# An mLSTM layer and its gated MLP on one core: score banks 2 and 3 for 2 and 5, an early table load, opening decays in three pieces, another order

## The chip, the cores and the metric

The program runs on one core of a Trainium2 chip. A core has five engines that run side by side and meet at semaphores: TensorE (PE in the profile; its weight loads are PEld), VectorE (DVE), ScalarE (ACT), GpSimd (POOL) and SyncE (SP), which here issues nearly all DMAs. The metric is the device time of one execution in microseconds (us), less is better. TensorE's clock has two levels, 1.2 and 2.4 GHz; the profile shows as "PEclk" which share of full speed was granted.

## The reference

```python
# mLSTM, for 4 batches x 8 heads, 768 tokens, head size 40
m_new = max(f[t] + m, i[t])
f_stab, i_stab = exp(f[t] + m - m_new), exp(i[t] - m_new)
C = f_stab * C + i_stab * outer(v[t], k[t])
n = f_stab * n + i_stab * k[t]
y[t] = sigmoid(o[t]) * (C @ q[t]) / max(abs(n @ q[t]), 1)
# then an MLP over all 3072 tokens: x is y with its 8 heads side by side (320 wide)
h = x @ w_in            # 320 -> 2048
out = (h * sigmoid(h)) @ w_out   # 2048 -> 320
```

## The kernel before

The sequence is cut into 6 chunks of 128 tokens, so there are 24 **units** (chunk c of batch b is unit n = 4c + b). A unit computes the mLSTM of its chunk in matrix form: scores of queries and keys, multiplied ("weighed") by a table of decays, times values, plus queries times the state that the chunk before left. The result is normalised, gated, and transposed into x. The MLP runs in eleven groups: an **opening** for units 0 to 3 (its pieces are called mA, mB and mJ, with tanh, glu and second product beside them), and ten **steps** of two units each, cut into 8 slices. First products are made of bits high and low (xh, xl, wh, wl) in fp32r. The weights come as 64-bit numbers and are put together on ACT and DVE (L329 to L386) before they are of use.

**The order is a table.** Nothing is scheduled at run time: the string ORDER holds some 1,600 words, and perform() calls one function for each, so that every engine gets its instructions in the order of the words. Each engine then runs its own list strictly in order, and an instruction that waits holds up all behind it. The words that matter here, with their lines before:

- z: spins, matmuls of 512 columns whose result nobody reads (L927).
- s, sb: the opening decays of units 0 to 3 in PSUM (spread L526, spans L543 and L553), e: their exponential (L564).
- S: scores (L657), w: weigh, DVE's product of the two score banks with the decay table D (L676), v and P: weighted values and their products with the keys (L594, L621), c: the state carried on (L637 to L643), V and Q: values and queries (L686, L705), g: gate (L722 to L736), x, h, y: transposes and the split into xh and xl (L742, L752, L756).
- m, a, b, f, F, n: a slice's first product (L769), tanh on ACT (L877), glu on DVE (L881), high part on ACT (L888), low part on DVE (L892), second product (L907). In the opening a, b, n are L815, L820, L831.
- qk, kvo, lq, d: the DMAs of a unit's queries and keys (raw, L470), of its keys, values and gate (kvo, L479), of its decays for queries (lq, L502) and of its decay table (D, L490). gs, gu, gm, gt, gf: gates (scan, sub, sum, top, flip), go: their store to DRAM (LFd, L276), from which lq and D are read back. t: tanh of the output gate on ACT (L610), O: a step's output copied from PSUM on ACT (L918), D: the output's DMA (L788).

PSUM has 8 banks of 512 columns. Before, second products gather in banks 0 and 1, first products alternate between banks 3 and 4, a unit's two halves of scores stand in **banks 2 and 5**, its transposes in 2, and banks 6 and 7 hold values, queries and products. The score banks are read by weigh as one operand, made by this function:

```python
def banks(a, b):
    return PS[:, a : b + 1 : b - a, :]     # for (2, 5): PS[:, 2:6:3, :]
```

Of the kernel before, what the change touches and what calls it, by code (L numbers as in the profile page):

```python
# [14 lines left out]
AF = mybir.ActivationFunctionType  # L15
# [40 lines left out]
kvo4 Mi5 Ri3 kvo5 Mo2 mB0 Zi2 k5.1 Ji2 aB0 Ti2 qk4 bB0 Ri2 mJ6 mJ4 lq6 So2 aJ6 Mo3 bJ6 So3 Si5 k5.0 aJ4 k6.0 mB2 aB2 nB0
bJ4 k6.1 e4.1 Zo3 Zo2 bB2 Jo2 mJ7 e4.0 Mc4 Sc4 aJ7 mB1 Li6 Lo5 Lo4 qk5 Zc4 Jo3 kvo6 gs2 aB1 e6.0 Mi4 nB2 l4 nJ4 nJ6 Jc4
bJ7 bB1 Zi5 Si4 Lo6 Lo7 Ji5 Zi4 mB3 Ji4 aB3 Ti5 e5.1 nJ7 Li7 mJ5 gu2 v4 Tc4 S4.0 e5.0 aJ5 Rc4 Mo5 lq5 Ri5 Mi6 P4 bB3 bJ5
S4.1 nB1 nJ5 v5 Ti4 mJ11 w4 t5 mJ10 Ri4 Si6 q4 qk6 Zi6 Mo4 Ji6 So5 lq7 c4 So4 nB3 Zo4 Zo5 P5 V4 aJ10 bJ10 aJ11 t4 bJ11
e6.1 S5.0 gm2 Ti6 Q4 Jo4 Mi7 gt2 Jo5 S5.1 g4 Si7 l5 Mo6 So6 Zi7 v6 l6 Ri6 q5 c5 mJ8 d7 gl Mo7 nJ11 q6 w5 go2 qk7 nJ10  # L60
k7.1 aJ8 k7.0 mJ13 Zo6 gf2 P6 aJ13 V5 e7.1 So7 Ji7 kvo8 S6.0 Ti7 Q5 bJ8 Ri7 S6.1 mJ12 Jo6 g5 bJ13 w6 Zo7 nJ8 aJ12 x4 Jo7
bJ12 d8 mJ9 h4 aJ9 y4 bJ9 x5 l7 mJ14 h5 nJ13 aJ14 e7.0 lq8 mJ15 kvo7 uh0 t7 nJ12 gs3 y5 ul0 bJ14 aJ15 k8.0 m1.0 uh1 nJ14
bJ15 ul1 a1.0 v7 b1.0 m1.1 uh2 c6 nJ9 t6 nJ15 O2 m1.3 a1.1 P7 b1.1 O0 V6 f1.1 ul2 S7 f1.0 O1 F1.0 a1.3 k8.1 b1.3 Q6 d9
m1.5 F1.1 m1.4 e8.1 O3 q7 a1.5 n1.0 uh3 qk8 qk9 b1.5 w7 g6 n1.1 f1.3 f1.5 kvo9 ul3 k9.0 gu3 e8.0 D2 c7 F1.3 k9.1 v8 m1.2
e9.0 x6 n1.3 uh4 t8 h6 y6 l8 P8 V7 F1.5 d10 a1.4 b1.4 ul4 uh5 S8 e9.1 k10.0 Q7 a1.2 m1.6 ul5 q8 b1.2 w8 g7 n1.5 f1.4
F1.4 f1.2 x7 uh6 ul6 m1.7 v9 h7 qk11 a1.6 y7 n1.4 c8 P9 V8 S9 F1.2 Q8 D1 uh7 a1.7 b1.6 f1.6 m2.0 F1.6 w9 gm3 b1.7 a2.0
f1.7 g8 ul7 n1.6 go3 n1.2 b2.0 m2.1 lq10 F1.7 a2.1 qk10 f2.0 gt3 x8 b2.1 D0 kvo11 D3 F2.0 kvo10 n1.7 m2.2 m2.3 t10 O4
f2.1 lq9 F2.1 lq11 l9 k10.1 O5 D4 a2.2 a2.3 e10.0 t9 b2.2 h8 f2.2 b2.3 lq12 c9 n2.0 m2.4 e10.1 m2.5 q9 n2.1 F2.2 a2.4
b2.4 v10 f2.3 t11 m2.6 f2.4 y8 d11 n2.2 F2.3 gf3 P10 F2.4 V9 S10 Q9 l10 w10 n2.4 d12 k11.1 a2.5 b2.5 k11.0 g9 l11 k12.1
f2.5 n2.3 F2.5 kvo12 a2.6 m2.7 x9 n2.5 b2.6 f2.6 e11.1 h9 y9 e11.0 F2.6 a2.7 b2.7 f2.7 F2.7 m3.1 lq13 m3.0 a3.0 v11 b3.0  # L70
n2.6 n2.7 c10 q10 a3.1 D5 b3.1 m3.2 O7 f3.0 f3.1 O6 D7 P11 F3.0 qk12 V10 S11 w11 Q10 g10 m3.3 n3.0 F3.1 q11 a3.2 k12.0
a3.3 d13 D6 b3.2 x10 b3.3 m3.4 c11 f3.2 h10 F3.2 e12.0 f3.3 F3.3 a3.4 y10 n3.1 l12 n3.2 k13.1 l13 b3.4 e12.1 v12 P12
f3.4 V11 S12 Q11 k13.0 e13.1 F3.4 w12 m3.5 m3.6 g11 a3.5 n3.3 c12 a3.6 kvo13 e13.0 t12 b3.5 x11 qk13 f3.5 F3.5 d14 b3.6
h11 y11 n3.4 m3.7 f3.6 a3.7 n3.5 lq15 m4.0 F3.6 b3.7 a4.0 n3.6 v13 b4.0 f3.7 F3.7 f4.0 m4.1 k14.1 a4.1 n3.7 O8 k14.0
lq16 F4.0 P13 b4.1 e14.1 O9 V12 f4.1 q12 S13 Q12 m4.2 c13 lq14 a4.2 w13 l14 m4.3 n4.0 F4.1 n4.1 b4.2 a4.3 g12 t13 b4.3
# [28 lines left out]
def mlstm_mlp_kernel(  # L104
# [95 lines left out]
    class Gates:  # L200
# [247 lines left out]
    class Unit:  # L448
# [606 lines left out]
```

## Time and profile before

| what | value |
|---|---|
| median of 3 runs | 489.66 us (487.79 to 490.27) |
| the profiled execution | 487.61 us, its span 485.7 us |
| PE busy | 460.3 us (95% of the span) |
| DVE, ACT, POOL busy | 265.2, 208.9, 89.4 us |
| mean granted clock | 0.979 |

The span is from the first to the last instruction; the rest of the execution's time, 1.9 us, lies around it. A matmul's busy time covers its pipelined end, so a PE that is busy all the time may still run at the low clock; the granted clock tells which. Idle time of an engine is put down to what ended it.

### The profile page before, as it was taken

The page shows a single profiled execution, that of the slowest core. Times are in us where ns is not written, and L with a number is a line of the kernel's source. Part 1 is how long each engine was busy: PE and PEld are TensorE (multiplying, and loading weights), DVE is VectorE, ACT ScalarE, POOL GpSimd, SP SyncE. Part 2 cuts the span into 40 slices and gives each one's busy share as a digit, 9 for nine tenths or more (in the row PEclk, how much of TensorE's full clock was granted, in tenths as well). Part 3 has the DMA queues.
Part 4 walks back from the last instruction along what each step waited for, and adds up shares of the span by engine and source line. Part 5 has one row for each costly group of instructions (what it writes and reads, how often), then busy time and mean ns, then how long its engine had stood idle before and what let it go on. Part 6 is the DMA issues. An engine that isn't in the chain of part 4 may idle for free.

```text
span 485.7 us, 13668 instructions
## 1 busy us (share of the span) xinstructions
PE 460.3 (95%) x5834; PEld 421.9 (87%) x5834; DVE 265.2 (55%) x537; ACT 208.9 (43%) x484; POOL 89.4 (18%) x126
## 2 busy tenths in 40 slices
PE   6998999999999889999989999899987999999997
PEld 3667687878989889999989999899987999999997
DVE  4478898883366544465365374445545445354432
ACT  2433565534553172463353534533461544423422
POOL 4221410411023020323113013030213011100000
PEclk9877999999999989999999999999999999999999
DMA  6747994230131512114035043124232022000000
GB/s 174 216 140 266 260 306 176 65 118 1 38 117 44 180 51 73 49 50 119 17 103 158 30 126 111 29 65 108 56 129 64 1 77 70 2 16 15 20 8 28
DMA packets 25149, 44.63 MB, mean 92 GB/s; under 512 B 3264, under 2 KB 15488, under 8 KB 25088
## 3 DMA queue, kind: packets, MB, share of 16 engines
q1 hardware_dynamic: 25024, 43.68, 29.9%
q8 instruction: 46, 0.75, 0.7%
q14 instruction: 15, 0.12, 0.1%
q10 hardware_dynamic: 64, 0.07, 0.0%
HBM read 39.71 MB, written 4.03 MB: 90 GB/s over the span
## 4 chain that ended last, share of the span: by engine, by line
PE 70%; issue 10%; DVE 7%; DMA 6%; POOL 3%; ACT 2%; SPq 1%; POOLq 0%; ACTq 0%; DVEq 0%
PE psum L769 32%; PE psum L907 23%; PE psum L831 4%; DMA D<-LFd 2%; PE psum L621 2%; DVE D L676 2%; PE psum L657 2%; PE psum L686 2%; DMA kvo<-in_kvo_dram 1%; PE psum L705 1%; PE psum L742 1%; POOL qt L607 1%; PE psum L833 1%; DMA LFd<-G 1%; POOL D L580 1%
## 5 line engine op out<-in xcount | busy, mean ns | idle before, releaser
L907 PE MATMUL psum<-woh,g 128*128 128x320 f32 x640 | 153.9, 313 | 5.8 <-DVE g L892 3.1
L907 PEld LDWEIGHTS psum<-woh,g 128*128 128x128 f32 x640 | 109.8, 188 | 7.6 <-DVE g L892 4.0
L907 PE MATMUL psum<-wol,g 128*128 128x320 f32 x320 | 99.0, 309 | 0.0
L877 ACT ACTIVATE th<-psum 128x512 f32<-128x512 f32 x80 | 47.4, 596 | 119.6 <-PE psum L769 86.1
L769 PE MATMUL psum<-xh,wh 128*128 128x256 f32 x480 | 87.3, 290 | 7.6 <-DVE D L676 7.4
L881 DVE SCALAR_TENSOR_TENSOR th<-th,psum 128x512 f32<-128x512 f32 x80 | 54.6, 684 | 67.0 <-ACT th L877 66.4
L769 PE MATMUL psum<-xl,wh 128*128 128x256 f32 x480 | 83.6, 282 | 0.0
L769 PEld LDWEIGHTS psum<-xh,wh 128*128 128x128 f32 x480 | 69.9, 190 | 10.6 <-DVE D L676 8.9
L892 DVE TENSOR_TENSOR g<-th,g 128x512 fp32r<-128x512 f32 x80 | 58.5, 735 | 34.5 <-ACT g L888 34.0
L769 PEld LDWEIGHTS psum<-xl,wh 128*128 128x128 f32 x480 | 68.9, 190 | 0.2 <-DVE xl L756 0.2
L888 ACT CAST g<-th 128x512 fp32r<-128x512 f32 x80 | 48.9, 617 | 45.6 <-DVE th L881 32.7
L769 PE MATMUL psum<-xh,wl 128*128 128x256 f32 x320 | 64.5, 283 | 0.0
L907 PEld LDWEIGHTS psum<-wol,g 128*128 128x128 f32 x320 | 60.4, 189 | 0.0
L580 POOL TENSOR_SCALAR_AFFINE_SELECT D<-D 64x512 f32<-64x512 f32 x40 | 31.9, 799 | 108.0 <-DMA D<-LFd 104.7
L769 PEld LDWEIGHTS psum<-xh,wl 128*128 128x128 f32 x320 | 49.8, 190 | 0.0
L574 ACT ACTIVATE D<-D,aT 128x64 f32<-128x64 f32 x160 | 42.0, 339 | 3.9 <-POOL D L580 3.9
L607 POOL TENSOR_TENSOR qt<-raw,eq 104x512 f32<-104x512 f32 x24 | 31.5, 1314 | 43.2 <-ACT eq L603 40.0
L642 POOL TENSOR_TENSOR S<-S,eq 104x164 f32<-104x164 f32 x20 | 10.3, 516 | 155.1 <-DVE S L640 135.6
L769 PE MATMUL psum<-X,wh 128*128 128x512 f32 (+1 forms) x120 | 32.2, 383 | 2.4 <-DVE D L676 1.6
L676 DVE TENSOR_TENSOR D<-psum,D 128x512 f32<-128x512 f32 x24 | 16.5, 689 | 26.9 <-PE psum L657 14.5
L769 PEld LDWEIGHTS psum<-X,wh 128*128 128x128 f32 x120 | 20.9, 196 | 7.7 <-DVE D L676 1.7
L831 PE MATMUL psum<-wo,g0J 128*128 128x320 f32 x72 | 21.4, 433 | 0.0
(123 smaller groups left out, 523.1 us busy)
## 6 DMA issues: line engine op xcount, KB each, us to landing
kvo<-in_kvo_dram SPq DMA_DIRECT2D x24, 484.0 KB
raw<-in_qk_dram SPq DMA_DIRECT2D x48, 160.0 KB
wro<-in_w_out_dram SPq DMA_DIRECT2D x8, 640.0 KB
D<-LFd SPq DMA_DIRECT2D x40, 128.0 KB
wri<-in_w_in_dram SPq DMA_DIRECT2D x8, 512.0 KB
lq<-LFd SPq DMA_DIRECT2D x48, 80.0 KB
out_dram<-ob SPq DMA_DIRECT2D x24, 160.0 KB
wrc<-in_w_in_dram SPq DMA_DIRECT2D x4, 256.0 KB
```

The lines of the kernel that those rows point to most:

```text
L574: nc.scalar.activation(d[:, j, :], e[:, j, :], AF.Exp, bias=aT[:, self.c, hf, r : r + 1])
L580: nc.gpsimd.affine_select(out=d, in_=d, compare_op=ALU.is_ge, fill=NEG, base=0, pattern=[[0, H], [1, LB]], channel_multiplier=-1,)
L607: nc.gpsimd.tensor_tensor(out=self.qt, in0=self.q[:KP], in1=self.eq, op=ALU.mult)
L642: nc.gpsimd.tensor_tensor(out=S2, in0=S1, in1=fd[1], op=ALU.mult)
L676: nc.vector.tensor_tensor(out=d, in0=self.ps, in1=d, op=ALU.mult)
L769: nc.tensor.matmul(ph, w, x, start=(i == 0), stop=(i == len(ops) - 1))
L831: nc.tensor.matmul(self.po[u][:, :DM], gs, w, start=(fc == 0), stop=last)
L877: nc.scalar.activation(th, self.ph[s], AF.Tanh, scale=0.5)
L881: nc.vector.scalar_tensor_tensor(out=th, in0=th, scalar=1.0, in1=ph, op0=ALU.add, op1=ALU.mult)
L888: nc.scalar.copy(t[:, 0], self.th[s])
L892: nc.vector.tensor_tensor(out=gl, in0=self.th.pop(s), in1=gh.bitcast(F32), op=ALU.subtract)
L907: nc.tensor.matmul(self.po[t], g[:, ts], w, start=(fc == 0 and i == 0), stop=(last and i == len(ops) - 1),)
```

## The change

1. The first products move to banks 4 and 5, the score banks become **2 and 3**, and the banks that hold opening decays, flips and opening transposes move along (3 becomes 4, 4 becomes 5, 5 becomes 3). banks(a, b) is now the plain slice PS[:, a : b + 1, :].
2. An ACTIVATE of one column comes first of all on ACT; it reads and writes the column that the spins read. The table load goes with it.
3. The opening decays come in three words, s, sp (the spans) and sb (the keys), where s and sb did it before; the last piece (L553) is a word of its own.
4. ORDER is new from end to end. It has 64 spins, before 24. From step 2 on most words stand where they stood, or a few places away; up to step 1 most stand elsewhere.

```diff
     def banks(a, b):
 
-        return PS[:, a : b + 1 : b - a, :]
+        return PS[:, a : b + 1, :]
...
-            ps = (2, 5) if n < WIDE or n > DONE else (5, 5)
-            px = 3 + n % 2 if n < 2 else 5 if n <= DONE else 2
+            ps = (2, 3) if n < WIDE or n > DONE else (3, 3)
+            px = 4 + n % 2 if n < 2 else 3 if n <= DONE else 2
...
-        return PS[:, 4 - turn[0], :]
+        return PS[:, 5 - turn[0], :]
...
-z7*4 s1 Lc0 gs0 Mc0 gu0 gm0 s0 gs1 kvo0 qk0 Sc0 Zc0 go0 gt0 z7*3 sb0 gu1 Jc0 gm1 S0 gt1 e0 Li0 lq0 lq1 qk1 kvo1 v0 lq2
+Li0 z7*5 s0 s1 gs0 gu0 Li1 kvo0 gm0 go0 z7*11 sp0 sp1 qk0 t0 gt0 sb0 gs1 gu1 Mi0 gm1 e0 lq0 Mi1 Lc0 kvo1 Si0 l0 lq1 gs2
...
     nc.vector.memset(busy, 1.0)
+    nc.scalar.activation(busy, busy, AF.Copy)
     perform(ORDER)
```

Three places of the order follow. The first is DVE at the start: the gates of the first chunk (L214 to L249; L249 is gt, the last of them, on which sb0 waits), and the putting together of the first weights (L337, L344). Before:

```order
L238 TENSOR_SCALAR G<-G 48x128
L243 SCALAR_TENSOR_TENSOR G<-keep,G 48x128
L214 SCALAR_TENSOR_TENSOR G<-G 48x128
L337 TENSOR_SCALAR wtc_156<-wtc_156 128x512
L344 SCALAR_TENSOR_TENSOR wtc_156<-wrc_152,wtc_156 128x512
L249 SCALAR_TENSOR_TENSOR G<-G 48x128
```

And of the change:

```order
L238 TENSOR_SCALAR G<-G 48x128
L243 SCALAR_TENSOR_TENSOR G<-keep,G 48x128
L249 SCALAR_TENSOR_TENSOR G<-G 48x128
L214 SCALAR_TENSOR_TENSOR G<-G 48x128
L229 TENSOR_TENSOR G<-G 48x128
```

gt0 no longer stands behind the weights, whose first instruction needs a DMA and a pass of ACT.

The second place is SP's queue of DMAs at the end of step 1 and the start of step 2, around the loads of units 10 and 11 and the store of the late gates (LFd from lml, go3). Before, from that store on; kvo_2145 is unit 10's:

```order
L276 DMA LFd<-lml 16x6x64
L276 DMA LFd<-lml 16x6x64
L502 DMA lq_137<-LFd 40x2x256
L502 DMA lq_137<-LFd 40x2x256
L470 DMA raw_134<-in_qk_dram 40x1024
L470 DMA raw_134<-in_qk_dram 40x1024
L788 DMA out_dram<-ob_1567 128x320
L479 DMA kvo_2141<-in_kvo_dram 128x968
L788 DMA out_dram<-ob_1673 128x320
L479 DMA kvo_2145<-in_kvo_dram 128x968
```

And of the change, up to that store; kvo_2192 is unit 10's:

```order
L479 DMA kvo_2006<-in_kvo_dram 128x968
L792 DMA out_dram<-ob_1633 128x320
L502 DMA lq_137<-LFd 40x2x256
L502 DMA lq_137<-LFd 40x2x256
L792 DMA out_dram<-ob_1631 128x320
L490 DMA D_2139<-LFd 64x2x256
L490 DMA D_2139<-LFd 64x2x256
L502 DMA lq_138<-LFd 40x2x256
L502 DMA lq_138<-LFd 40x2x256
L479 DMA kvo_2192<-in_kvo_dram 128x968
L502 DMA lq_136<-LFd 40x2x256
L502 DMA lq_136<-LFd 40x2x256
L276 DMA LFd<-lml 16x6x64
```

The store moved from ahead of both units' loads to behind them.

The third place is DVE in step 7 at unit 20's weigh (L676 before, L680 after), here with the semaphores that an instruction waits for. Before:

```order
L892 TENSOR_TENSOR g_5_3972<-th_5_3969,g_5_3972 128x512 [waits Activation_49]
L640 TENSOR_TENSOR S_0_121<-S_0_121,psum 104x164 [waits Pool_49]
L643 TENSOR_TENSOR S_1_122<-S_1_122,psum 104x164 [waits Pool_49]
L676 TENSOR_TENSOR D_3380<-psum,D_3380 128x512 [waits PE_49,Activation_49]
L881 SCALAR_TENSOR_TENSOR th_6_3991<-th_6_3991,psum 128x512 [waits DVE_49]
```

And of the change:

```order
L885 SCALAR_TENSOR_TENSOR th_5_4010<-th_5_4010,psum 128x512 [waits Activation_49]
L896 TENSOR_TENSOR g_4_3942<-th_4_3904,g_4_3942 128x512
L680 TENSOR_TENSOR D_3425<-psum,D_3425 128x512
L885 SCALAR_TENSOR_TENSOR th_6_4032<-th_6_4032,psum 128x512 [waits PE_49,Activation_49]
L896 TENSOR_TENSOR g_5_4013<-th_5_4010,g_5_4013 128x512 [waits PE_49]
```

Before, this weigh waits for PE and for ACT; in the change it waits for neither.

## Rows read from the trace of the kernel before

**Rows 1.** The page, busy time and share of each engine.

```profile
PE 460.3 (95%) x5834; PEld 421.9 (87%) x5834; DVE 265.2 (55%) x537; ACT 208.9 (43%) x484; POOL 89.4 (18%) x126
```

**Rows 2.** Windows: length, busy PE, PEld, DVE, ACT, POOL, granted clock, DMA.

```profile
3.60:36.40 32.80, 28.95 (x578) 17.95 (x571) 19.83 (x47) 12.12 (x22) 8.88 (x12) 0.84 0.63 187
36.40:54.65 18.25, 16.70 (x162) 13.17 (x161) 15.85 (x34) 7.83 (x16) 4.44 (x5) 0.81 0.77 248
54.65:114.80 60.15, 58.95 (x571) 46.64 (x570) 48.71 (x89) 31.06 (x75) 12.90 (x15) 1.00 0.53 165
200.00:430.00 230.00, 219.70 (x3045) 214.37 (x3044) 114.25 (x237) 102.15 (x248) 45.48 (x60) 1.00 0.25 72
```

**Rows 3.** Waits of PE, whole span: us in total, times, longest.

```profile
PE psum L769 <- DVE D L676: 8.9, 11, 2.1
PE psum L907 <- ACT ob L918: 2.7, 2, 2.0
```

**Rows 4.** Line L676 (weigh): what it waited for, then who waited for it.

```profile
  PE psum L769: 7.0, 4
...
  ACT th L877: 13.8, 3
...
  PE psum L769: 8.9, 11
```

**Rows 5.** Timeline, step 7 at unit 19: start, us, engine, line; idle before in brackets.

```profile
354.67 0.69 DVE L676 TENSOR_TENSOR D<-psum,D 128x512 f32<-128x512 f32 x1
355.41 0.62 PE L769 MATMUL psum<-xh,wh 128*128 128x256 f32 x3 [2.07 <-DVE D L676]
```

**Rows 6.** Timeline, step 7 at unit 20.

```profile
372.97 2.49 POOL L607 TENSOR_TENSOR qt<-raw,eq 104x512 f32<-104x512 f32 x2
373.11 0.69 DVE L676 TENSOR_TENSOR D<-psum,D 128x512 f32<-128x512 f32 x1 [2.85 <-PE psum L769]
373.72 2.29 DVE L892 TENSOR_TENSOR g<-th,g 128x512 fp32r<-128x512 f32 x1
...
376.07 0.56 PE L907 MATMUL psum<-woh,g 128*128 128x320 f32 x2 [2.70 <-DVE g L892]
```

**Rows 7.** Timeline, end of step 1 and start of step 2.

```profile
159.26 0.79 SPq L276 DMA_DIRECT2D LFd<-lml  x2
...
163.16 0.33 SPq L479 DMA_DIRECT2D kvo<-in_kvo_dram  x1
...
170.16 0.47 ACT L610 ACTIVATE kvo<-kvo 128x320 f32<-128x320 f32 x1 [5.60 <-DMA kvo<-in_kvo_dram]
...
171.01 0.41 PE L907 MATMUL psum<-woh,g 128*128 128x320 f32 x1 [2.03 <-ACT ob L918]
...
172.38 0.41 PE L907 MATMUL psum<-woh,g 128*128 128x320 f32 x1 [0.66 <-ACT ob L918]
```

**Rows 8.** Windows, the stretch just behind (columns as in rows 2).

```profile
172.40:177.20 4.80, 4.80 (x25) 4.80 (x26) 3.02 (x5) 4.04 (x13) 2.52 (x4) 0.64 0.29 89
```

**Rows 9.** Timeline of the head.

```profile
6.25 1.28 ACT L329 ACT_TABLE_LOAD   x1 [6.25 <-DMA wrc<-in_w_in_dram]
...
9.69 1.13 PE L553 MATMUL psum<-minus,G 16*64 16x256 f32 x8 [3.06 <-issue]
...
15.40 1.20 ACT L603 ACTIVATE eq<-lq 104x512 f32<-104x512 f32 x2 [0.22 <-DMA lq<-LFd]
...
22.70 1.08 PE L705 MATMUL psum<-S,qt 40*64 40x41 f32 x16
...
24.95 3.17 PE L927 MATMUL psum<-G 128*128 128x512 bf16 x7
...
32.72 1.04 PE L927 MATMUL psum<-G 128*128 128x512 bf16 x4
...
35.98 0.63 PE L769 MATMUL psum<-X,wh 128*128 128x256 f32 x3
```

**Rows 10.** Groups by line, DVE's costliest: busy us, mean ns of one.

```profile
L892 DVE TENSOR_TENSOR g<-th,g 128x512 fp32r<-128x512 f32 x80 | 58.5, 735 | 34.5 <-ACT g L888 34.0
```

More of the change, by code (lines that the diff above doesn't have):

```diff
@@ L56 @@
[L56 to L75, printed above, removed]
@@ new lines @@
+mB2 mJ7 Ti5 k4.1 Jc4 Lo6 aB2 Tc4 e4.1 aJ7 nJ5 bB2 Li7 nJ4 bJ7 Mi4 Si4 e4.0 Ri5 Mo4 l4 Rc4 mJ10 aJ10 v4 mB1 lq5 bJ10 t4
+nB2 So4 Zi4 Ji4 w4 nJ7 Mo5 aB1 qk5 k5.1 bB1 Zo4 P4 k5.0 Ti4 Ri4 So5 V4 lq6 mJ8 mB3 go2 aJ8 Mi6 e5.0 k6.0 bJ8 nB1 mJ11
+Jo4 Si6 aB3 nJ8 k6.1 Mo6 Zo5 e6.0 bB3 Zi6 Lo7 d7 aJ11 mJ9 e5.1 c4 Jo5 nJ10 gl kvo6 Ji6 aJ9 Mi7 l5 bJ11 q4 So6 v5 k7.0
+Ti6 l6 Zo6 nB3 Q4 S5.0 q5 Ri6 P5 S5.1 bJ9 t5 mJ12 nJ11 mJ13 e6.1 Mo7 qk6 Si7 nJ9 g4 w5 c5 V5 S6.0 Q5 aJ12 bJ12 lq7 Zi7
+Ji7 S6.1 v6 d8 So7 k7.1 Ti7 kvo7 Jo6 nJ12 t6 q6 w6 Ri7 mJ15 g5 x4 gs3 aJ13 h4 P6 lq8 bJ13 y4 aJ15 bJ15 Zo7 kvo8 qk9 V6
@@ new lines @@
+lq23 k21.1 f7.2 m7.4 a7.3 c19 x18 F7.2 b7.3 lq21 f7.3 e20.1 h18 k21.0 kvo21 m7.5 v20 a7.4 e21.1 l21 b7.4 n7.2 t19 P20
+t20 F7.3 V19 y18 S20 d22 lq22 Q19 a7.5 f7.4 g19 b7.5 n7.3 m7.6 D15 f7.5 F7.4 k22.1 w20 F7.5 m7.7 n7.5 x19 k22.0 a7.6
+a7.7 h19 b7.6 b7.7 f7.6 e21.0 y19 n7.4 F7.6 m8.0 a8.0 v21 m8.1 b8.0 kvo22 e22.1 f7.7 f8.0 c20 F7.7 n7.6 m8.2 a8.1 F8.0
+n7.7 a8.2 b8.1 P21 V20 S21 w21 q20 Q20 m8.3 f8.1 F8.1 O16 e22.0 O17 n8.0 b8.2 g20 a8.3 qk22 t21 f8.2 x20 b8.3 d23 m8.4
+f8.3 n8.1 h20 t22 qk23 m8.5 k23.0 F8.2 v22 a8.4 c21 F8.3 b8.4 y20 n8.2 k23.1 P22 l22 e23.0 V21 S22 a8.5 b8.5 q21 Q21
@@ L100 @@
+F10.2 a10.4 b10.3 f10.3 n10.1 b10.4 F10.3 n10.2 f10.4 m10.5 n10.3 a10.5 m10.6 b10.5 f10.5 F10.4 a10.6 F10.5 m10.7 n10.4
+b10.6 f10.6 a10.7 n10.5 b10.7 f10.7 F10.6 F10.7 n10.6 n10.7 D21 O22 D22 O23 D23
 """
@@ L256, in flip @@
             s = self.cols(c, n)
-            pt = PS[:, 5 if 0 < c < 3 else 2, : n * 2 * NB].rearrange("p (c h r) -> p c h r", h=2, r=NB)
+            pt = PS[:, 3 if 0 < c < 3 else 2, : n * 2 * NB].rearrange("p (c h r) -> p c h r", h=2, r=NB)
             for k in range(n):
@@ L518, in spread @@
         def spread(self):
-            a, b = (0, 1) if self.n % 2 == 0 else (3, 4)
+            a, b = (0, 1) if self.n % 2 == 0 else (4, 5)
             self.e = banks(a, b)[:, :, : HF * LB].rearrange("p f (j t) -> p f j t", t=LB)
@@ L532, in spread, with cell @@
                         )
-        def spans(self):
-            cell = lambda r, hf: (
+        def cell(self, r, hf):
+            return (
                 slice(r * 64, (r + 1) * 64), slice(32 * hf, 32 * hf + NB),
@@ L538, in spans @@
             )
+        def spans(self):
             for j in range(HF):
@@ L541, in spans @@
                     for hf in range(2):
-                        out, rows, at, x = cell(r, hf)
+                        out, rows, at, x = self.cell(r, hf)
                         nc.tensor.matmul(
@@ L549, in spans, with keys @@
                         )
+        def keys(self):
             for r in range(2):
                 for hf in range(2):
-                    out, rows, at, x = cell(r, hf)
+                    out, rows, at, x = self.cell(r, hf)
                     nc.tensor.matmul(
@@ L925, in spin @@
     def spin(k, bank):
+        bank = {3: 4, 4: 5, 5: 3}.get(bank, bank)
         for _ in range(k):
@@ L967, in mlstm_mlp_kernel @@
     UNIT = dict(qk="load_raw", kvo="load_kvo", d="load_d", lq="load_lq", s="spread", e="exps",
-                k="mask", sb="spans", v="column", l="decay", q="scaled", t="opened",
+                k="mask", sp="spans", sb="keys", v="column", l="decay", q="scaled", t="opened",
                 P="products", c="carry", S="scores", w="weigh", V="values", Q="queries",
```

64 lines of the change are left out of this document (36 added, 28 removed).

## The prediction

> **What bounds the kernel now.** I read the page's busy shares first: PE is busy 95% of the span [rows 1], so the time is PE's work plus what PE loses. I then cut the span into stretches [rows 2]. Between 54.65 and 114.80 us PE is idle for 60.15 - 58.95 = 1.2 us only, at full clock: nothing can be won there but an earlier start. The losses lie in three other places, and the list of PE's waits names most of what ended them [rows 3].
>
> *In the steps.* From 200 to 430 us PE is idle 230.0 - 219.7 = 10.3 us [rows 2]. Most of it is the first product (L769) waiting for weigh (L676): 8.9 us in 11 waits [rows 3], of which one is the head's only idle between 36.40 and 54.65 (18.25 - 16.70 = 1.55 us [rows 2]); 8.9 - 1.55 = 7.4 us remain for ten waits in the steps. The longest shows what it is: weigh runs from 354.67 to 355.36 and the first product starts at 355.41, after 2.07 us of idle PE [rows 5]. But this first product writes bank 3 or 4, and weigh reads banks 2 and 5. They share nothing. The order's table of dependencies must have taken the slice 2:6:3 as all that lies from 2 to 5. The same holds the other way: four weighs waited 7.0 us for a first product, and three tanhs (L877, which read bank 3 or 4) waited 13.8 us for a weigh [rows 4]. What that does to PE is seen once: at 373.11 a weigh has waited 2.85 us for a first product; the low part behind it on DVE is late, and PE waits 2.70 us for that at 376.07 [rows 6]. 7.4 + 2.7 is nearly all of the 10.3 us.
>
> *At step 2.* Unit 10's kvo is issued at 163.16, its tanh starts at 170.16, and ACT waited 5.60 us for that DMA. Behind the tanh on ACT stands the copy of step 1's output, which frees the banks for step 2's second product: PE waits 2.03 us and then 0.66 us [rows 7]. The clock falls: 4.80 us at a granted mean of 0.64 [rows 8], which is 4.80 x 0.36 = 1.7 us more.
>
> *In the head.* The first product that counts starts at 35.98 [rows 9]. DVE is idle 32.80 - 19.83 = 13.0 us of the time up to 36.40 and 18.25 - 15.85 = 2.4 us up to 54.65, and PE ran at a mean granted clock of 0.84 and 0.81 in the two [rows 2].
>
> **The change part by part, against the 487.6 us of the profiled execution** (the median is 2.0 us above it; runs of this kernel differ by 0.5%, about what can be told from no change).
>
> *Banks 2 and 3.* A plain slice of two neighbours covers nothing else, and the first products now use 4 and 5. The order's third place shows a weigh whose waits for PE and ACT are gone. So the ten waits in the steps go, up to 7.4 us, and the 2.70 us at 376 with them. Bounds: nothing, if whatever comes next on PE waits for the same DVE or ACT; 10.1 us, all of it. From step 2 on the words stand nearly as before, several second products stand between a first product and what needs it, and DVE has 114 of 230 us to do [rows 2], so little should come in their place. I take the whole 10.1 here and put what comes back into a term of its own.
>
> *Loads at step 2.* The store of the late gates (159.26 [rows 7]) waited for DVE at the head of SP's queue, and lq, raw and two kvo's were issued in a bunch behind it within 4 us. Now it stands behind both units' loads, and unit 11's kvo and unit 10's lq come a slice earlier. What is late next is the store itself, but its readers are the units of chunk 3, from 12 on. If kvo lands before ACT comes to the tanh, 2.03 + 0.66 + 1.7 = 4.4 us go. Bounds: 0, if the transfers still bunch; 4.4. I take 4.4, since the queue is now unblocked by some 3 to 4 us and the two PE waits are shorter than that.
>
> *The head.* Three things happen. The table load of 1.28 us, which waited for a weight's DMA at 6.25, leaves the path of the first gates; gt0 stands before the weights, so the 3.06 us that PE waited until 9.69 for sb0 shrink [rows 9]. 40 more spins are to keep the clock up. And Q0 stands earlier: its decays land at 15.4 [rows 9], ACT takes 0.6 us (1.20 for two [rows 9]) and POOL 1.25 (2.49 for two [rows 6]), so the queries are ready near 17.3, but PE comes to them at 22.70 [rows 9], behind other units' scores and decays at half clock. I followed the new lists of DVE and POOL by hand: state and queries of unit 0 done at about 18 to 19, Q0 at 19 to 20, Q1 at 24 to 25, the last split of unit 1's x at about 30, against 36.4. Behind that DVE is nearly full (15.85 of 18.25 us [rows 2]) and has about as many instructions before the opening's big pieces as now, so of the 6 us I count 4. Bounds: 0 (DMA lands no earlier: the store of the first gates is issued as early, but now behind three bigger loads) and 8 (half of the 13.0 + 2.4 us that DVE is idle). From 54.65 on PE is full, and what the head wins stays won.
>
> *The splitting of the decays* adds no instruction. *The added ACTIVATE* costs ACT nothing on the path; but all spins read the column that it writes, so they now wait for the table load, to about 2.6 us instead of 0.93. Nothing else on PE can start before 2.75 in this trace (the spread waits for POOL), so this hides; without that cover it would be 1.7 us.
>
> *What comes back.* Step 1 is ordered anew and tighter: between unit 5's transposes and the first product that needs them stands one second product of the opening now, before there were four pieces, against a copy on ACT, a subtraction on DVE and whatever stands ahead of them. I put 1 us there and 1.5 us for new waits elsewhere; bounds 0 and 5.4 (twice the 2.7 us that PE waits for output copies now [rows 3]).
>
> Sum: 10.1 + 4.4 + 4.0 - 2.5 = 16.0; 487.6 - 16.0 = 471.6, say **472 us**.
>
> **Where POOL speaks against it.** While POOL multiplied the queries (372.97, 2.49 us for two), the low part on DVE took 2.29 us [rows 6], against a mean of 0.735 [rows 10]: 1.55 us more. The Trainium skill says the same in "SBUF — State Buffer", section "Who interferes with whom": VectorE's second pair of ports is GpSimd's, an exclusive lock, and a DVE instruction with two SBUF inputs waits for a GpSimd instruction that reads SBUF. By that rule, and this row agrees, engines that are let loose meet more often.
>
> **The rivals.**
>
> 1. *The waits move.* PE no longer waits for weigh, but DVE and POOL now meet where PE has no slack: five such meetings on the path cost 5 x 1.55 = 7.8 us, and the time is 472 + 7.8 = 480. For it: that row. Against: the mean of 0.735 us over 80 low parts says that few meet.
> 2. *The spins cost more than they give.* Seven spins took 3.17 us at the low clock, 0.45 each, four took 1.04 us, 0.26 each, once it was up [rows 9]. 45 spins stand ahead of Q0. Should the clock stay low, that is 45 x 0.45 = 20 us on PE from 2.6 us on, with some 10 us of real work between: Q0 at 33 in place of 22.70, and where I counted 4 us won, some 7 are lost: 472 + 4 + 7 = 483. Against: PE has no gap there that could bring the clock down.
> 3. *More in the head.* DVE follows at once and half of its idle goes (8), nothing comes back, and most of the clock's loss up to 54.65 (18.25 x 0.19 = 3.5 us [rows 2]) is saved beside it, say 3: 472 - 4 - 2.5 - 3 = 462.
> 4. *Slower: loads run late.* In step 1 and after, decay tables and kvo's were shuffled on SP, whose queue also holds the fences between values and queries. One load that lands late costs 4.4 us, as at step 2 now. It decides from four on (16.0 / 4.4 = 3.6); with five the time is 472 + 22 = 494. For it: ACT's wait of 5.60 us [rows 7]. Against: DMA is used to a quarter there [rows 2].
> 5. *No change.* The head gains nothing and a new stall like that of step 2, with a few waits behind weigh, eats the rest: 485 to 490.
>
> **How the numbers follow.** My forecast has a chance of 0.60, with 464 to 478 as its own range (terms of 10.1, 4.4 and 4 at their ends, not all at once). Rival 1 has 0.17, rival 2 0.08, rival 3 0.05, rival 4 0.05, rival 5 0.05. A range from 463 to 483 takes in my forecast, rival 1 and half of rival 2: 0.81. Faster by over 0.5%: 0.60 + 0.17 + 0.08 + 0.05 = 0.90; the same 0.05; slower 0.05.
>
> **What would show it.** In the new profile, PE's waits for DVE's D should be gone from the first product's line, and weigh's from the first product. Between 160 and 180 no wait for the output's copy, and a full clock. The first product that counts should start near 30, the window from there to 55 should show a clock near 1. From 200 to 430 PE should be idle under 3 us. I am wrong if that window still has 8 us of idle under other names, if the first product starts after 35, or if step 1 shows a wait of several us.

## The result, and the profile after

The changed kernel takes **467.73 us** (466.73 to 473.41, 4 runs) against 488.73 us of the kernel before on the same chip: a ratio of 0.960, with a 95% interval of 0.951 to 0.969. The profiled execution took 468.0 us, its span is 466.2 us, its mean granted clock 0.992. The forecast was 472, with 463 to 483.

The page after, busy time and share of each engine, as in [rows 1]:

```profile
PE 454.5 (98%) x5874; PEld 417.9 (90%) x5874; DVE 268.6 (58%) x537; ACT 207.8 (45%) x485; POOL 89.8 (19%) x126
```

PE is busy 5.8 us less, though it runs 40 more spins, and 98% of the span. The windows of the kernel after, with the columns of [rows 2]:

```profile
3.60:36.40 32.80, 29.33 (x490) 15.52 (x489) 18.02 (x48) 7.99 (x17) 6.27 (x10) 0.90 0.55 171
36.40:54.65 18.25, 16.74 (x295) 12.90 (x294) 17.18 (x36) 8.78 (x19) 3.67 (x4) 1.00 0.71 188
...
150.00:200.00 50.00, 50.00 (x696) 49.26 (x698) 25.62 (x51) 22.84 (x54) 10.94 (x14) 1.00 0.23 72
200.00:430.00 230.00, 230.00 (x3121) 226.62 (x3113) 121.12 (x252) 104.43 (x252) 42.93 (x55) 1.00 0.24 72
```

From 150 to 430 us PE is never idle: the 10.3 us of idle time in [rows 2] and the output copy's stall of [rows 7] are gone, and so is the low clock of [rows 8]. The list of PE's waits, total, times and longest, which answers to [rows 3]:

```profile
PE psum L932 <- DVE S L647: 3.2, 1, 3.2
PE psum L932 <- ACT G L982: 2.7, 1, 2.7
PE psum L932 <- DVE D L680: 1.5, 1, 1.5
```

L773 is now the first product, L680 weigh, L932 the spins. No first product waits for weigh any more. The waits that are left, but for a few tenths, are those of spins, and they stand in the head. Weigh's own line shows the other side, as in [rows 4]:

```profile
its engine sat idle before it (us, times) until:
  PE psum L661: 22.6, 9
  ACT ob L854: 1.7, 1
who waited for it (us, times):
  PE psum L932: 1.5, 1
```

Weigh waits for its own scores (L661), which it must, and no more for first products; no tanh waits for it, and the only thing on PE that waits for it is a spin. But the head did not come out as forecast. PE in the timeline of the kernel after, as in [rows 9]:

```profile
16.65 0.64 PE L545 MATMUL psum<-G,ident 16*64 16x64 f32 x32
20.46 4.00 PE L932 MATMUL psum<-G 128*128 128x512 bf16 x9 [3.17 <-DVE S L647]
24.39 0.61 PE L260 MATMUL psum<-ident,G 16*128 16x16 f32 x2
...
27.18 0.68 PE L625 MATMUL psum<-vw,kvo 64*64 64x41 f32 x32
27.67 0.66 PE L690 MATMUL psum<-kvo,D 64*64 64x41 f32 x32
...
28.59 0.66 PE L709 MATMUL psum<-S,qt 40*64 40x41 f32 x16
...
39.91 0.59 PE L932 MATMUL psum<-G 128*128 128x512 bf16 x2 [1.51 <-DVE D L680]
40.16 0.70 PE L773 MATMUL psum<-X,wh 128*128 128x256 f32 x3
```

Unit 0's queries (L709) start at 28.59, before at 22.70 [rows 9]; the first product that counts starts at 40.16, before at 35.98. Where the parts of the kernel start in each trace (us; the first matmul of the part, found by counting the matmuls of the order's words). Runs 1, 2 and 6 are told below:

| start of | before | the change | run 1, banks alone | run 2, order alone | run 6, spins in free banks |
|---|---|---|---|---|---|
| first product that counts | 36.0 | 40.2 | 36.9 | 46.4 | 33.1 |
| step 1 | 114.8 | 118.0 | 113.4 | 125.4 | 112.9 |
| step 2 | 155.0 | 153.4 | 152.8 | 161.3 | 148.3 |
| step 3 | 195.9 | 189.2 | 188.6 | 198.9 | 185.6 |
| step 8 | 379.7 | 361.6 | 361.1 | 378.3 | 357.9 |
| last second product | 480.6 | 461.1 | 460.6 | 480.2 | 457.5 |

By this table the change wins 1.6 us up to step 2, 5.1 in step 2, and 12.8 from step 3 to the last second product: 19.5 of the 19.6 us between the two profiled executions.

### The profile page after: what moved, and what is told of

It reads as the page before. It is cut to its first block, busy times and chain, and to the rows that moved or that the text cites. A ratio compares the mean times of both kernels' runs of the same rounds, so it can differ in the third digit from the quotient of the medians.

```text
span 466.2 us, 13740 instructions
## 1 busy us (share of the span) xinstructions
PE 454.5 (98%) x5874; PEld 417.9 (90%) x5874; DVE 268.6 (58%) x537; ACT 207.8 (45%) x485; POOL 89.8 (19%) x126
## 4 chain that ended last, share of the span: by engine, by line
PE 83%; ACT 1%; issue 0%
PE psum L773 37%; PE psum L911 30%; PE psum L835 3%; PE psum L625 2%; PE psum L661 2%; PE psum L709 2%; PE psum L690 2%; PE psum L746 1%; PE psum L837 1%; PE psum L838 1%; ACT D L578 0%; PE psum L260 0%; ACT wto L329 0%; PE psum L749 0%; PE psum L265 0%; ACT wti L329 0%
## 5 line engine op out<-in xcount | busy, mean ns | idle before, releaser
L911 PE MATMUL psum<-woh,g 128*128 128x320 f32 x640 | 152.8, 311 | 0.0
L773 PE MATMUL psum<-xh,wh 128*128 128x256 f32 x480 | 86.5, 288 | 0.0
L773 PE MATMUL psum<-xl,wh 128*128 128x256 f32 x480 | 83.1, 281 | 0.0
L896 DVE TENSOR_TENSOR g<-th,g 128x512 fp32r<-128x512 f32 x80 | 59.7, 754 | 26.4 <-ACT g L892 25.6
L773 PEld LDWEIGHTS psum<-xh,wh 128*128 128x128 f32 x480 | 69.5, 188 | 1.2
L773 PEld LDWEIGHTS psum<-xl,wh 128*128 128x128 f32 x480 | 68.6, 189 | 0.0
L773 PE MATMUL psum<-xh,wl 128*128 128x256 f32 x320 | 64.2, 282 | 0.0
L773 PEld LDWEIGHTS psum<-xh,wl 128*128 128x128 f32 x320 | 49.4, 188 | 0.0
L646 POOL TENSOR_TENSOR S<-S,eq 104x164 f32<-104x164 f32 x20 | 9.3, 464 | 168.0 <-DVE S L644 129.4
L611 POOL TENSOR_TENSOR qt<-raw,eq 104x512 f32<-104x512 f32 x24 | 32.9, 1375 | 12.1 <-ACT eq L607 11.7
L773 PE MATMUL psum<-X,wh 128*128 128x512 f32 (+1 forms) x120 | 31.1, 374 | 0.4 <-ACT wto L329 0.4
L680 DVE TENSOR_TENSOR D<-psum,D 128x512 f32<-128x512 f32 x24 | 16.5, 687 | 24.4 <-PE psum L661 22.6
L932 PE MATMUL psum<-G 128*128 128x512 bf16 x64 | 20.0, 454 | 7.7 <-DVE S L647 3.2
L773 PEld LDWEIGHTS psum<-X,wh 128*128 128x128 f32 x120 | 20.2, 188 | 5.0 <-issue 0.8
```

The lines of the kernel that those rows point to most:

```text
L611: nc.gpsimd.tensor_tensor(out=self.qt, in0=self.q[:KP], in1=self.eq, op=ALU.mult)
L680: nc.vector.tensor_tensor(out=d, in0=self.ps, in1=d, op=ALU.mult)
L773: nc.tensor.matmul(ph, w, x, start=(i == 0), stop=(i == len(ops) - 1))
L896: nc.vector.tensor_tensor(out=gl, in0=self.th.pop(s), in1=gh.bitcast(F32), op=ALU.subtract)
L911: nc.tensor.matmul(self.po[t], g[:, ts], w, start=(fc == 0 and i == 0), stop=(last and i == len(ops) - 1),)
L932: nc.tensor.matmul(PS[:, bank, :], busy.broadcast_to([128, 128]), busy.broadcast_to([128, 512]), start=True, stop=True,)
```

## The experiments

Theory: the score banks' slice was taken as all four banks from 2 to 5, the waits that followed from it are the gain, and the new order adds the rest at step 2 and in the head. Rivals: the order brings the gain, or the loads at step 2 do.

**Run 1, the banks alone.** The kernel before, its order untouched, with the new banks:

```diff
-        return PS[:, a : b + 1 : b - a, :]
+        return PS[:, a : b + 1, :]
...
-            ps = (2, 5) if n < WIDE or n > DONE else (5, 5)
-            px = 3 + n % 2 if n < 2 else 5 if n <= DONE else 2
+            ps = (2, 3) if n < WIDE or n > DONE else (3, 3)
+            px = 4 + n % 2 if n < 2 else 3 if n <= DONE else 2
```

> The kernel before with the new banks alone: score banks 2 and 3, first products in 4 and 5, the old order and the old start. Theory (the slice from bank 2 to 5 made first products, tanhs and weighs wait for each other): PE's ten waits for weigh in the steps (7.4 us) and the 2.7 us at 376 go, the wait of the store at step 2 shortens a little; 10 to 13 us faster, 474 to 478 against 487 to 489. Rival (the new order brought the gain): under 4 us faster, since the old order still makes PE come to the same places at the same time.

Measured: 468.04 us (467.01 to 469.42), a ratio of 0.960 (0.955 to 0.965). That is the whole gain, and more than the 10 to 13 us that were expected of it. Two windows of its profile, columns as above:

```profile
150.00:200.00 50.00, 50.00 (x722) 49.09 (x720) 26.18 (x55) 22.00 (x52) 10.38 (x13) 1.00 0.29 90
200.00:430.00 230.00, 230.00 (x3088) 226.70 (x3081) 121.28 (x253) 104.27 (x252) 42.37 (x55) 1.00 0.25 71
```

The stall at step 2 is gone as well, though the store of the late gates still stands ahead of the loads. SP's DMA issues and ACT in this run's timeline:

```profile
154.68 0.80 SPq L276 DMA_DIRECT2D LFd<-lml  x2
...
158.58 0.33 SPq L479 DMA_DIRECT2D kvo<-in_kvo_dram  x1
```

```profile
164.38 0.47 ACT L610 ACTIVATE kvo<-kvo 128x320 f32<-128x320 f32 x1 [2.85 <-DMA kvo<-in_kvo_dram]
```

The store (L276) is issued at 154.68, before at 159.26 [rows 7], unit 10's kvo at 158.58 in place of 163.16, and its tanh (L610) runs at 164.38 in place of 170.16. Some 2.2 us of this is the whole kernel being earlier; the rest is DVE's. In the kernel before, the last pass of the late gates (L243), which makes what the store sends, stood behind a weigh that waited for a first product. DVE in the timeline of before:

```profile
157.20 0.69 DVE L676 TENSOR_TENSOR D<-psum,D 128x512 f32<-128x512 f32 x1 [2.28 <-PE psum L769]
...
158.19 1.05 DVE L243 TENSOR_TENSOR_SCAN lml<-keep,lfi 48x128 f32<-48x128 f32 x3
```

So the stall at step 2 was a child of the same wait.

**Run 2, the order alone.** The changed kernel with the old banks:

```diff
-        return PS[:, a : b + 1, :]
+        return PS[:, a : b + 1 : b - a, :]
...
-        return PS[:, 5 - turn[0], :]
+        return PS[:, 4 - turn[0], :]
```

> The changed kernel with the old banks (2 and 5, first products in 3 and 4); new order, early table load and the three-piece decays stay. Theory: the waits of first products for weigh come back and with them some 10 us: 476 to 481. Rival (the order brought the gain): 468 to 471.

Measured: 486.96 us, a ratio of 1.000 (0.997 to 1.003). PE's waits, and the steps' window:

```profile
PE psum L773 <- DVE D L680: 5.1, 9, 1.3
PE psum L931 <- DVE S L647: 3.6, 2, 2.5
```

```profile
200.00:430.00 230.00, 222.72 (x3071) 217.46 (x3071) 115.16 (x239) 102.07 (x249) 46.07 (x59) 1.00 0.24 72
```

The first product waits for weigh again, nine times, and PE is idle for 7.3 us in the steps. Over the whole kernel the new order and the early table load bring nothing by themselves. Neither expectation held, though, and the order is not idle: by the table above the first product that counts starts 10.4 us later than before, and this is won back by the end.

**Run 3, the slice alone.** The kernel before, its banks 2 and 5 and its order kept, but with weigh as two instructions of one bank each, so that no operand spans banks:

```diff
-            nc.vector.tensor_tensor(out=d, in0=self.ps, in1=d, op=ALU.mult)
+            for f in range(2):
+                nc.vector.tensor_tensor(out=d[:, f], in0=self.ps[:, f], in1=d[:, f], op=ALU.mult)
```

> The kernel before, its banks 2 and 5 kept, but weigh in two instructions of one bank each: no operand spans banks 3 and 4 any more, while DVE has one instruction more for each of 24 units. Theory: first products no longer wait for weigh, as with new banks; DVE pays 24 times about 0.15 us, mostly hidden; 474 to 480. Rival (the waits come from the place of weigh in the order or from real use of a bank): no faster than before, 487 to 491.

Measured: 468.84 to 469.38 us in three executions, a ratio of 0.962 (0.955 to 0.970), and no idle PE from 200 to 430 us: nearly the gain of run 1 (468.04), with no bank moved, and more than was expected. What counts is which banks an operand is taken to cover, not how many instructions read them.

**Run 4, the store alone.** The kernel before, with its old banks, and only the store of the late gates (go3) moved behind unit 11's lq:

```diff
-n1.6 go3 n1.2 b2.0
+n1.6 n1.2 b2.0
...
-F2.1 lq11 l9
+F2.1 lq11 go3 l9
```

> The kernel before with one word moved: the store of the late gates (go3) behind the loads of units 10 and 11 on SP's queue. Theory: unit 10's kvo is issued some 3 us earlier, PE's 2.0 and 0.7 us at 171 and 172 and the clock's loss of 1.7 us go: 4 us faster, 483 to 485. Rival (the transfers bunch whatever the queue does, or the loads wait for buffers): within 1.5 us of before.

Measured: 485.62 us, a ratio of 0.995 (0.992 to 0.998), about 2.4 us faster, between the two expectations. At step 3 it was 5.6 us ahead of the kernel before (190.3 against 195.9), 4.6 of them won in step 2, so the prediction's term for the loads was real and of the right size. But 3.8 us of it were lost in step 7. PE's row of its timeline, and DVE's just before:

```profile
372.67 0.56 PE L912 MATMUL psum<-woh,g 128*128 128x320 f32 x2 [3.47 <-DVE g L897]
```

```profile
368.95 0.69 DVE L681 TENSOR_TENSOR D<-psum,D 128x512 f32<-128x512 f32 x1 [2.85 <-PE psum L774]
369.56 3.06 DVE L897 TENSOR_TENSOR g<-th,g 128x512 fp32r<-128x512 f32 x1
```

The weigh (L681) waits 2.85 us for a first product, as in [rows 6], and the low part behind it (L897) takes 3.06 us while POOL multiplies the queries (369.59, 2.47 us for two), where one takes 0.735 on the mean [rows 10]. PE waits 3.47 us for that, before it was 2.70. This is 0.8 us of the 3.8. The rest is the clock. In run 4 it fell twice, behind a first product's wait of 2.07 us for a weigh, which ended at 349.77, and behind the wait above:

```profile
350.00:360.00 10.00, 10.00 (x69) 10.00 (x69) 4.06 (x7) 5.79 (x17) 1.07 (x2) 0.83 0.26 88
370.00:380.00 10.00, 7.33 (x43) 7.29 (x44) 5.61 (x6) 2.89 (x8) 2.06 (x2) 0.83 0.00 0
```

A granted clock of 0.83 in two windows of 10 us is 3.4 us; with the 0.8 that is a little more than was lost. In the kernel before, PE waits at the same two places (2.07 and 2.70 us, [rows 5, 6]), and the granted clock of both windows is 1.00. So the won time was lost where the false waits are, most of it through the clock; why the clock fell here and not before stays open.

**Run 5, the waiting spins left out.** The changed kernel without the fifteen spins that the trace showed waiting (a spin's result is read by nobody):

```diff
-c0 z7*9 gf2 v1 z7*4 gf1 sb2
+c0 gf2 v1 gf1 sb2
...
-So0 v3 z2*2 mA0
+So0 v3 mA0
```

> The changed kernel without the fifteen spins of the head that were seen waiting: nine and four ahead of the late gates' flips (bank 7, in which unit 0's values and keys still stood) and two ahead of the first product (bank 2, unit 3's scores). Nothing that the output needs is left out. In the changed kernel's profile they waited 3.17 and 1.51 us and ran 4.00, 1.05 and 0.25 us; queries of unit 0 at 28.59, first product that counts at 40.16, 467.7 us. Theory (these spins are why the head came late, and what the head wins stays won): queries of unit 0 at 24 to 25, first product at 36 to 37, and the end 3 to 4 us earlier, about 464. Rival A (the head is bound by DVE, 17.18 of 18.25 us busy up to 54.65): first product earlier by 2 us or more, end within 0.7 us of 467.7. Rival B (the spins are wanted, they keep the clock up): pieces of scores take 1.1 in place of 0.69 us up to the first product, end later, 469 to 472.

Measured: 469.13 us (467.25 to 469.55), a ratio of 0.962 (0.957 to 0.966): no gain. Six rows of PE's timeline show why:

```profile
15.50 0.69 PE L661 MATMUL psum<-raw 40*64 40x64 f32 x32
...
16.36 0.64 PE L545 MATMUL psum<-G,ident 16*64 16x64 f32 x32
19.34 0.60 PE L260 MATMUL psum<-ident,G 16*128 16x16 f32 x2 [2.34 <-DVE G L249]
...
22.36 1.09 PE L625 MATMUL psum<-vw,kvo 64*64 64x41 f32 x32
...
28.49 1.14 PE L661 MATMUL psum<-raw 40*64 40x64 f32 x32
...
40.00 0.62 PE L773 MATMUL psum<-X,wh 128*128 128x256 f32 x3
```

PE is idle for 2.34 us at 19.34, since the flips wait for gates on DVE. After that a piece of scores or products takes 1.1 us where it took 0.69 at 15.50, up to 37 us, and the granted clock from 3.6 to 36.4 us is 0.71. Rival B held: those spins were wanted, at that place.

**Run 6, the same spins in free banks.** They run, but write banks 4 and 0, which nothing reads then:

```diff
-c0 z7*9 gf2 v1 z7*4 gf1 sb2
+c0 z3*9 gf2 v1 z3*4 gf1 sb2
...
-So0 v3 z2*2 mA0
+So0 v3 z0*2 mA0
```

(The word's bank 3 is mapped to 4 in the function of the spins.)

> The changed kernel with the same fifteen spins written into banks that nothing reads at that time (4 and 0), so that they run but do not wait. Theory that the wait is the harm: the 3.17 us at 20.46 and the 1.51 us at 39.91 are gone, the nine spins take 9 x 0.21 = 1.9 in place of 4.00 us since no gap of 3 us lets the clock fall ahead of them; queries of unit 0 near 25, first product near 37, 464 to 465. Rival A (DVE bounds the head): first product at 37 to 39, end within 0.7 us of 467.7. Rival B (what stands behind the spins waits for the same thing): PE waits there under another name for as long, and nothing moves, first product at 40.

Measured: **463.74 us** (462.74 to 464.97), a ratio of 0.952 (0.947 to 0.956). The same place of PE's timeline:

```profile
16.18 0.63 PE L545 MATMUL psum<-G,ident 16*64 16x64 f32 x32
16.75 2.14 PE L932 MATMUL psum<-G 128*128 128x512 bf16 x8
19.16 0.39 PE L260 MATMUL psum<-ident,G 16*128 16x16 f32 x2 [0.27 <-DVE G L249]
...
21.69 0.68 PE L625 MATMUL psum<-vw,kvo 64*64 64x41 f32 x32
...
23.11 0.66 PE L709 MATMUL psum<-S,qt 40*64 40x41 f32 x16
...
33.10 0.73 PE L773 MATMUL psum<-X,wh 128*128 128x256 f32 x3
```

No wait, no low clock: spins fill the gap until the flips can run at 19.16, unit 0's queries are at 23.11 and the first product at 33.10, 7.1 us earlier than in the change. At step 1 5.1 us of this are left, at step 3 3.6. One wait of spins is left behind the first product, 1.2 us at 36.56 for another carried state (L647).

**Run 7, no spins at all.** Run 1's kernel (old order, new banks) without its 24 spins:

```diff
-z7*4 s1 Lc0 gs0
+s1 Lc0 gs0
...
-z7*3 sb0 gu1
+sb0 gu1
```

(and four more words of that kind)

> The kernel before with the new banks and without its 24 spins (their result is read by nobody). With the spins it took 468.04 us; its first product came at 36.9, and until 28 its pieces of scores took 1.13 us, from 30 on, behind five spins in a row, 0.69. Theory (spins buy clock, and the head needs it): pieces stay near 1.1 us up to and into the first products; some eight pieces of 0.4 us more from 30 to 37, and as much behind, 471 to 474. Rival (PE is not the bound of the head, DVE and POOL are): first product at 36 to 38, end within 1 us of 468.0. A third outcome, 466 or less, would say that the spins themselves stood in the way.

Measured: 467.66 us (466.95 to 468.25), a ratio of 0.960 (0.955 to 0.964), where run 1 had 468.04. The rival held. PE in its timeline, and the waits:

```profile
27.95 1.14 PE L657 MATMUL psum<-raw 40*64 40x64 f32 x32
...
36.11 1.00 PE L769 MATMUL psum<-X,wh 128*128 128x256 f32 x3
```

```profile
PE psum L742 <- DVE x L732: 2.8, 3, 1.8
```

Three first products take 1.00 us there and 0.62 in run 1, so by its durations PE is still at its low level, and the first product starts at 36.1 all the same, against 36.9. In the old order PE waits for DVE's normalised outputs (2.8 us in three waits). In the new order PE itself sets the head: between 21 and 37 us run 5's PE is never idle for more than 0.4 us, and its low level costs 6.9 us at the first product (40.0, against 33.1 in run 6).

**Run 8, the early table load without the new order.** Run 1's kernel with the ACTIVATE first of all, and gt0 ahead of the first weights:

```diff
-gm0 s0 gs1 kvo0 qk0 Sc0 Zc0 go0 gt0 z7*3
+gm0 gt0 s0 gs1 kvo0 qk0 Sc0 Zc0 go0 z7*3
...
+    nc.scalar.activation(busy, busy, AF.Copy)
     perform(ORDER)
```

> The kernel before with the new banks, the ACTIVATE that loads the table first of all, and gt0 moved ahead of the first weights on DVE: two things of the changed kernel's head without its order. In the kernel with the banks alone the keys' part of the opening decays (L553) came at 9.52 after a wait of 2.89 us, the table load at 6.09 to 7.38, the first product at 36.9, 468.04 us in all. Theory (the prediction's term for the head, its first two parts): the keys' part at 6.5 to 7, and 1 to 2 us of this stay to the end, 466 to 467. Rival (the chain of the head runs over the stored gates, which land at 9.9, and over POOL's queries, whose keys land at 14.9): the keys' part comes early, the first product at 36.5 to 37, end within 0.5 us of 468.0.

Measured: 469.04 us (467.54 to 471.83), a ratio of 0.964 (0.958 to 0.970): no gain over run 1, and neither expectation held whole. The keys' part ran at 7.86 in place of 9.52, the first product at 34.5 in place of 36.9, and step 1 started at 111.1 in place of 113.4. But step 3 started at 188.4 against 188.6. Three windows say where 2.1 us went:

```profile
160.00:165.00 5.00, 4.53 (x37) 4.27 (x36) 0.70 (x2) 2.32 (x6) 0.34 (x1) 1.00 0.40 134
...
175.00:180.00 5.00, 5.00 (x154) 4.56 (x153) 1.85 (x4) 0.00 (x0) 0.00 (x0) 0.92 0.01 3
180.00:185.00 5.00, 5.00 (x29) 5.00 (x28) 2.96 (x9) 2.70 (x7) 0.88 (x2) 0.74 0.53 161
```

PE was idle for 0.47 us, and the granted clock of 0.92 and 0.74 in the other two is 0.4 + 1.3 us more.

**Runs 9 to 11, on one chip.** The kernel of run 6 with one second product moved between the flips of the late gates and unit 10's products (run 9), the kernel of run 6 again (run 10), and the change again (run 11):

```diff
-F2.3 gf3 P10 F2.4 V9 S10 Q9 l10 w10 n2.2 n2.4
+F2.3 gf3 n2.2 P10 F2.4 V9 S10 Q9 l10 w10 n2.4
```

> The kernel with the fifteen spins in free banks, and one second product of step 2 (n2.2) moved ahead by eight words, so that it stands between the six flips of the late gates (gf3) and unit 10's values, queries and scores. With the free banks alone the profile showed 463.74 us, and from 174 to 177.7 a granted clock of 0.64, 0.50, 0.50 and 0.65 in slices of 1 us, with no idle PE, behind 1.6 us of flips and 2.3 us of small matmuls; in the changed kernel the same matmuls in the same order ran at 1.00. Theory (the thin stretch, flips and small matmuls in a row, can lower the clock, and full matmuls between them prevent it): 1.00 from 150 to 200, step 3's first product 1.5 us earlier than at 185.6, and 462 us. Rival A (the clock falls for a reason outside the program, now and then): the dip is there or not whatever the order, and the median stays within 0.5 us of the same kernel without the move. Rival B: unit 10's chain, which is 1.7 us later, makes a first product of step 3 wait, 464 to 465.

> The kernel with the fifteen spins in free banks as it was, beside the one above and the changed kernel on the same chip, since less than 1% stands between them. Theory that the head's win stays but for the clock's dip at step 3: 463 to 464, with the dip again in its profile and the first product that counts near 33. Rival: 466 to 468, the first measurement was a lucky chip.

> The changed kernel, unaltered, beside the two above on the same chip. Theory (the head's spins cost it 3 to 5 us): 467 to 468.5, first product that counts at 40, a wait of 3.2 us ahead of the nine spins. Rival: 464 to 465 here too, and the difference to the free banks is the chip's.

Measured: 463.39 us (462.78 to 464.37), ratio 0.949 (0.946 to 0.953); 463.59 us (462.51 to 465.31), ratio 0.950 (0.946 to 0.953); 468.78 us (466.54 to 473.15), ratio 0.961 (0.956 to 0.967). So the free banks are worth 1.1% over the change, with intervals that do not meet; the nine spins' wait of 3.2 us is there again in run 11's profile and absent from those of runs 9 and 10. Run 9 was made for this dip in run 6, in slices of 1 us:

```profile
174.00:175.00 1.00, 1.00 (x53) 0.92 (x45) 0.64 (x2) 0.00 (x0) 0.00 (x0) 0.64 0.00 0
175.00:176.00 1.00, 1.00 (x6) 1.00 (x5) 0.93 (x5) 0.00 (x0) 0.00 (x0) 0.50 0.06 16
...
177.00:178.00 1.00, 1.00 (x6) 1.00 (x6) 0.23 (x2) 0.00 (x0) 0.00 (x0) 0.65 1.04 180
```

PE is busy throughout, and the clock falls to its lower level, 1.2 GHz, for some 3 us. Run 10's profile shows the dip again, run 9's does not (1.00 from 150 to 200). Of ten executions with the order of run 6, three have a mean clock of 0.996 and take 464.4 to 465.3 us, the others 462.5 to 464.4; all six of run 9 have 1.0. Yet the medians differ by 0.2 us only, as rival A has it, so what the move is worth stays open.

## Why the prediction came out right

The total was 4 us too high, and the place of most of the gain was named rightly. The banks and what comes back were put too low, the head too high; and one of the prediction's own signs of being wrong, a first product "after 35", came true.

- **The banks, 10.1 us.** The mechanism is shown by runs 1, 2 and 3. The term was too small: from step 3 to the end the change won 12.8 us, and run 1, whose order there is the old one, 12.7. I had added up idle PE time, and a matmul's busy time hides the start of each wait. Two rows of the change's timeline:

```profile
174.15 0.52 PE L773 MATMUL psum<-xh,wh 128*128 128x256 f32 x3
174.51 0.40 PE L773 MATMUL psum<-xh,wl 128*128 128x256 f32 x2
```

  Three first products start 0.36 us before the next group, 0.12 each, but count as busy for 0.52: the last one's end hangs over by 0.16. Ten waits and the one at 376 in [rows 3, 6] hide 11 x 0.16 = 1.8 us, and 10.3 + 1.8 = 12.1 of the 12.7.
- **Loads at step 2, 4.4 us.** From step 2 to step 3 the change won 5.1 us, run 1 5.1, run 4 4.6. The size was right and the reason half right. I had taken the store's place in SP's queue as the cause; run 1 shows that the store was late because what it sends stood on DVE behind a weigh that waited. Either cure does, and they do not add up.
- **The head, 4.0 us.** This step failed. It said "Q0 at 19 to 20" and a first product "at about 30"; they came at 28.59 and 40.16, and the 1.6 us won up to step 2 are less than run 1's 2.2 without any of it. I had followed DVE and POOL by hand, and costed the spins only by the clock (rival 2, whose argument against, that PE has no gap there, was wrong). What I did not look at was which bank a spin writes. Nine of them wrote bank 7 while unit 0's keys and values stood there to be carried into its state (L647): they waited 3.17 us, the clock fell, and the nine took 4.00 us; in run 6, without a wait, 2.14 (eight of them have records). Two more waited 1.51 us for unit 2's weigh just ahead of the first product. Run 6 takes the waits away and is at 463.74, 4.0 us under the change's 467.73; side by side, in runs 10 and 11, it is 5.2. At step 2 run 6 stands 4.5 us ahead of run 1. The head had about what the term said, and the change did not collect it. But the spins' waits are not all that was wrong: without them, in run 6, unit 0's queries still come at 23.11, and not at 19 to 20. The flips wait there for DVE's gates until 19.16, and 4 us of PE's own list stand between them and the queries. That list I had not followed.
- **"What the head wins stays won."** Mostly: of 7.1 us at the first product in run 6 5.1 stay at steps 1 and 2 and 3.6 at the end of its profile; the 1.5 lost between go with the clock's dip at 174. Run 8 lost nearly all of its 2.3.
- **The early table load.** It came at 1.20 to 2.48 us and the spins started at 2.75, as the prediction said. That this hides is not shown: the spread (L526) stands behind five of the spins and started at 5.00, before at 2.75, and no run has the new order without the ACTIVATE. In the old order, with gt0, it moved the first product by 2.3 us (run 8).
- **What comes back, 2.5 us.** Nothing did: PE is busy for 50.00 of 50.00 and 230.00 of 230.00 us. Rival 1 had DVE and POOL meeting more often. The low part's group in the change, count, busy time and mean ns:

```profile
L896 DVE TENSOR_TENSOR g<-th,g 128x512 fp32r<-128x512 f32 x80 | 59.7, 754 | 26.4 <-ACT g L892 25.6
```

  Its mean rose from 735 ns [rows 10] to 754, which is 80 x 0.019 = 1.5 us of DVE, and PE waited for none of it. The Trainium skill's rule on the shared ports ("SBUF — State Buffer", section "Who interferes with whom") agrees with the sign. Its price on the path shows in the kernel before [rows 6] and in run 4, where a low part met POOL's queries just behind a weigh that was late: 2.29 - 0.735 = 1.55 us and 3.06 - 0.735 = 2.3 us. In the change PE's list of waits has no low part.

The sum, with what was measured from the profiled executions:

| term | predicted | measured |
|---|---|---|
| banks, in the steps | 10.1 | 12.8 |
| loads at step 2 | 4.4 | 5.1 |
| head and step 1 | 4.0 | 1.6 |
| what comes back | -2.5 | 0 |
| together | 16.0 | 19.5 |

Three terms were too low, by 2.7, 0.7 and 2.5 us, and the head was too high by 2.4. That the sum came out within 3.5 us is in part luck. Run 1 says more than the sum: one line of the change, with the bank numbers that go with it, is worth all of its gain; what the rest of the new order loses in the head and wins behind it about cancels. The Trainium skill ("PSUM — Partial Sum Buffer", section "PSUM bank collisions raise a hardware error") advises to guard PSUM by bank; by that rule a product in bank 3 or 4 needs no guard against a reader of banks 2 and 5. No sum rests on it; the two runs with and without the wide guard give its price here, 20 us.

## What to carry to other kernels

Look at which waits the program holds that the data do not ask for: a strided slice over banks 2 and 5 was tracked as all banks between, and its waits showed up far from it, in a late low part and in a late DMA store. Give a spin that only keeps the clock up a bank that nobody reads at the time, or it waits like any other write and takes the clock down with it. When adding up idle time from a profile, add the end of the last matmul that each wait hides.

## What the runs showed of the hardware that was not expected

- **The clock fell with PE busy.** In runs 6, 8 and 10 the granted clock fell somewhere between 174 and 185 us, to 0.50 in the finest slices, behind the flips (18 matmuls of 16 columns) and four groups of 32 small matmuls. In the change and in run 1 the same groups ran at 1.00. What decides it stays open.
- **Short gaps, large differences.** In run 5 a gap of 2.34 us of idle PE at 17 us was followed by pieces of 1.1 us up to 37 us; in run 6, with spins in that gap, they took 0.69.
- **The clock's row and the durations disagree in the head.** Run 7's row for 3.6 to 36.4 us says a granted clock of 1.00, while its 32 score matmuls took 1.14 us at 27.95, against 0.69 in run 6. The trace of run 7 holds no record of the clock before 45.58 us, and a window counts such a stretch as full. The first row of [rows 2] counts the time up to 16.26 us in that way too, though pieces took 1.13 us there [rows 9], so its 0.84 is too high. In the head the durations are to be read.
- **The clock scatters from run to run.** The six executions of run 11 took 466.5 to 473.2 us with mean granted clocks from 0.995 down to 0.982; the six of run 9 all had 1.0 and took 462.8 to 464.4.
